# Routed tokens of a two-stage mixture of experts: number and gate scattered as a pair, slot lists loaded as rows and turned by TensorE, token rows of 2048 bytes

## The chip, the cores and the metric

One core of a Trainium2 chip runs the whole kernel. The metric is the device time of one execution in microseconds (us). A run counts as the same when it is within 2% by the verdicts shown with results; the prediction says which smaller difference it holds to be measurable.

## The reference, cut to what matters

Linear attention over 4 x 8 heads gives x, 2304 tokens of 512. A first mixture of 8 experts weights every expert for every token. A second mixture, the part that the change touches, sends each token to one expert only:

```python
logits = xn @ en.T / tau
expert_idx = np.argmax(logits, axis=1)
gate_w = probs[np.arange(N), expert_idx]
for e in range(E):
    mask = expert_idx == e
    h = np.maximum(x[mask] @ w1[e], 0.0)
    out[mask] = gate_w[mask, None] * (h @ w2[e])
```

## The kernel before, in words

The work is written out by hand, in a fixed order on every engine. Attention comes first. Then the first mixture runs as 48 half-stages h, one for each of 16 halves of an expert and each of three batches of 768 tokens (bi = 0, 1, 2); the last three are h = 45, 46 and 47, and each of them finishes the sums of one batch. In the last stages a half-stage has 30 ticks: 14 of `p1_group` (first layer, reading x tiles `xT`, `xB`), then 16 of `p2_plain` (second layer, six matmuls of 384 columns each). Work beside it is hung on ticks: in the list `tail` (L1288 to L1298) tick k means tick k of h = 46 up to 39, and k counts from 40 at the start of h = 47.

**Routing.** Tokens are routed in batches t0 = 0, 6, 12 (in tiles of 128 tokens, six to a batch). For each tile, `route_l` (L883, matmuls L886) makes the logits and `route_a` (L872) turns the tile's sums into rows on TensorE (psum tile psB, one buffer), squares them for the norm and copies them to a row tile (both on ScalarE, L878 and L879). Then `route_b`, `route_o`, `route_c`, `route_s`, `route_d` and `route_w` (L889 to L954) find each token's expert, its slot in the expert's list and its gate. `route_w` writes the gate as element 513 of each row and has SyncE store the rows to `x2d` in DRAM, 513 floats to a token. `route_i` (L956) has GpSimd scatter a tile's token numbers (`tokid`) into the slot list `ids[i]`; there are six lists, one for each tile position i, which are filled beforehand so that the sum over the six is the token number, or NT for an empty slot.

**The table.** `first_blocks` and `other_blocks` (L1018, L1027) turn the counts into a table of blocks (128 slots of one expert): offset, expert, and whether the expert differs from the block before. The first six blocks (NEARLY = 6) are taken from the first two batches, the rest from all.

**The second mixture.** `second(0, 22)` (L1349) runs 22 blocks. For block i, SyncE reads three registers of the table (`load_regs`, L1044) and issues six list loads (`load_ids`, L1053, line L1058), each 128 numbers of 4 bytes, one to a partition. `gather` (L1060) adds the six columns on GpSimd (L1065 to L1067) and has GpSimd gather 128 rows of x2d (L1069) into one of two buffers `xgs`. `tx` turns them (L1111) and splits them into a high part `xth` (ScalarE) and a low part `xtl` (VectorE, L1115), and copies the gate out of the row (`gt`, L1117). `p1` is the first layer: 24 matmuls of 512 columns (L1131 to L1133). `relu` evacuates it (L1141), `th_` turns the hidden values (L1146) and splits them (`hTh` on ScalarE, `hTl` on VectorE, L1150), `p2` is the second layer, 24 matmuls (L1164 to L1166), scaled by the gate into y (L1171) and scattered by GpSimd (L1172).

Weights come in eight chunks of 512 KB for each block, w1 and w2. `wcond` (L1071, line L1074) issues a chunk's load, which moves nothing where the expert is the same. `wsplit` (L1094) casts a chunk on ScalarE (`s1h`, `s2h`, L1102; the last chunk of w2 on GpSimd, L1100) and takes the low half on VectorE (`s1l`, `s2l`, L1103), 1024 columns each. Then the raw tile is free, and the next block's `wcond` of that chunk is issued right after: SyncE's queue follows VectorE's splits. `load_raws` issues the first block's eight chunks; `first_w1(i, cs)` splits w1 chunks of block i and issues those of block i + 1.

The loop of `second` writes, for block i from 2 on, in this order: `p1(i)`; w1 splits of block i + 1; `relu(i)`; `tx(i + 1)`; w2 splits of block i, each followed by `wcond` of block i + 1; for i = 3 alone the rest of the table and `load_ids(6)`; `p2(i - 1)`; `gather(i + 3)`; `th_(i)`. From i = 4 on `load_ids(i + 3)` stands at the head of the turn. Every engine goes through its own part of this order without overtaking.

Of the kernel before, what the change touches and what calls it, by code (L numbers as in the profile page):

```python
# [22 lines left out]
NT = B * S  # L23
# [19 lines left out]
XW = 513  # L43


def build(tc, a, out):
# [30 lines left out]
    c0.tile([P, 16], F32, name="cpad")  # L77
# [10 lines left out]

    x2d = dr.tile([NT + 1, XW], F32, name="x2d")
    ids = [dr.tile([NSLOT, 1], I32, name=f"ids{k}") for k in range(RB)]  # L90
# [174 lines left out]
    sent = wp.tile([P, 1024], I32, tag="wS1_1", name="sent")  # L265
    sents = [sent[:, i * (NSLOT // P):(i + 1) * (NSLOT // P)] for i in range(2)]
    G.memset(sents[0], 0)
    G.memset(sents[1], NT)
    zrow = wp.tile([P, 1024], F32, tag="wA12_1", name="zrow")[0:1, 0:XW]
# [16 lines left out]
    def misc_comp():  # L286
# [4 lines left out]
        V.tensor_copy(iob, itmp3)  # L291
        V.memset(half, 0.5)
# [29 lines left out]
    def load_w(kind, n):  # L322
        if n >= NGR:
            return
        e, g = divmod(n, 2)
        rs = []
        for r_ in range(2):
            t = raw() if kind == 1 or n == 0 else live["h3"].tile([P, 1026 if r_ else 1024], F32, tag=f"rx{r_}", name=f"rx{n}_{r_}")[:, 0:1024]
# [391 lines left out]
    live["h3"].tile([P, 120], F32, name="hpad")  # L720
# [137 lines left out]
    def batch(t0):  # L858
        if t0 not in rt:
            if t0 == TPB:  # L860
                pieces = [live["h3"].tile([P, 2 * TH], F32, tag="r" + q_, name=f"rows{t0}{q_}").unsqueeze(1)[:, :, 0:XW] for q_ in "abcd"]
                pieces += [raw().unsqueeze(1)[:, :, 0:XW] for _ in range(2)]
            else:
                pieces = [live["h3"].tile([P, 2, XW], F32, tag=f"hT{k + 2}", name=f"rows{t0}_{k}") for k in range(TPB // 2)]
            m = TPB // len(pieces)
            rt[t0] = dict(n=TPB, ss=sm.tile([P, 6], F32, tag="ss", bufs=2, name=f"ss{t0}"), rows=[t[:, k] for t in pieces for k in range(m)], pieces=pieces)
        return rt[t0]
# [4 lines left out]
    def route_a(t0, i):  # L872
        r = batch(t0)
        row = r["rows"][i][:, 0:DM]
# [4 lines left out]
        A.copy(row, ps)  # L879

# [63 lines left out]
    def route_w(t0):  # L944
# [105 lines left out]
    idt, idr, xg = {}, {}, {}  # L1050
    xgs = []

    def load_ids(i):  # L1053
        if i not in regs:
            load_regs(i)
        idr[i] = c0.tile([P, RB], I32, tag="idr", bufs=5, name=f"idr{i}")
        for k in range(RB):
            SP.dma_start(out=idr[i][:, k:k + 1], in_=ids[k][bass.ds(regs[i][0], P), :])  # L1058

    def gather(i):  # L1060
        if not xgs:
            xgs.append(live["h3"].tile([P, 2, XW], F32, tag="rx1", name="xgs"))
# [43 lines left out]
    xsp, gt = {}, {}  # L1106

    def tx(i):
# [7 lines left out]
        gt[i] = c0.tile([P, 1], F32, tag="gt", bufs=4, name=f"gt{i}")  # L1116
        V.tensor_copy(gt[i], xg[i][:, DM:DM + 1])  # L1117
# [231 lines left out]
    def second(i0, i1):  # L1349
# [168 lines left out]
```

## Time and profile before

| | us |
|---|---|
| median of 3 runs (lowest, highest) | 2051.58 (2047.44, 2053.9) |
| the profiled execution, its own time | 2048.7 |
| its span in the trace | 2046.8 |
| TensorE busy | 1969.2 (96%) |
| VectorE, ScalarE, GpSimd busy | 1295.8, 869.2, 1055.7 |
| mean granted clock of TensorE | 0.987 |

Times in the rows are microseconds from the start of the span. PE is TensorE, PEld its weight loads, DVE VectorE, ACT ScalarE, POOL GpSimd, SPq the instructions by which SyncE issues DMAs. "[15.69 <-ACT rows L879]" says that the engine stood idle for 15.69 us before the row and which instruction ended that by the profile. A granted clock of 1.00 is 2.4 GHz, 0.50 is 1.2 GHz. The second mixture begins with the row of 1745.76 below and runs to the end; within it TensorE's two layers of one block take about 12.3 us.

### The profile page before, as it was taken

Reading aid. Unit: us, or ns where it says so; the run is one execution under the profiler, and the core shown is the slowest. Engines: PE = TensorE matmul, PEld = TensorE weight load, DVE = VectorE, ACT = ScalarE, POOL = GpSimd, SP = SyncE. Lnnn points to the kernel's source line nnn. Section 1 sums busy time; section 2 is a strip of 40 time slices with the busy share of each in tenths; the row PEclk is TensorE's granted clock in tenths of the full one; section 3 lists DMA queues with packets and bytes.
Section 4 is the critical chain, followed back from the end, with each engine's and each line's share of the span. In section 5 each row is a group of like instructions: output and inputs, shape, how many; then the busy total and the mean of one; then the engine's idle time right before and its main releaser. Section 6 shows DMA issues by size and latency. Waiting matters only on the chain.

```text
span 2046.8 us, 31493 instructions
## 1 busy us (share of the span) xinstructions
PE 1969.2 (96%) x11627; PEld 1888.7 (92%) x11627; DVE 1295.8 (63%) x1838; ACT 869.2 (42%) x1391; POOL 1055.7 (52%) x811
## 2 busy tenths in 40 slices
PE   9999999999999999999999999999999996799998
PEld 8999999999999999999999999999999995578886
DVE  6766556466656655655665665565566453689996
ACT  5566442223332433333342333334233232568785
POOL 1255112666574747656483756647384441345553
PEclk9999999999999999999999999999999997799999
DMA  4344643452725435372634537263543367434861
GB/s 121 111 146 166 227 160 149 141 199 100 249 92 194 157 124 190 108 253 80 212 135 146 180 104 245 85 229 115 166 166 120 119 147 114 63 113 136 298 227 64
DMA packets 138287, 314.63 MB, mean 154 GB/s; under 512 B 30456, under 2 KB 85256, under 8 KB 138130
## 3 DMA queue, kind: packets, MB, share of 16 engines
q1 hardware_dynamic: 134034, 302.06, 45.5%
q0 software_dynamic: 4096, 10.51, 1.7%
q8 instruction: 94, 1.54, 0.3%
q14 instruction: 63, 0.52, 0.1%
HBM read 335.81 MB, written 32.28 MB: 180 GB/s over the span
## 4 chain that ended last, share of the span: by engine, by line
PE 62%; POOL 11%; DVE 9%; issue 8%; DMA 6%; SPq 2%; ACT 2%; POOLq 0%; DVEq 0%; ACTq 0%
PE Q L427 14%; PE Q L426 14%; PE Q L428 14%; DMA rw<-in_moe_w 4%; POOL w1S L346 3%; PE psD L206 3%; DVE s2l L1103 2%; PE psD L426 2%; PE psD L427 2%; POOL hT L474 2%; PE psD L428 2%; PE psA L426 2%; PE psA L428 2%; PE psA L427 2%; POOL w1A L346 2%
## 5 line engine op out<-in xcount | busy, mean ns | idle before, releaser
L490 DVE TENSOR_TENSOR acca<-acca,Q 128x768 f32<-128x768 f32 x182 | 168.7, 951 | 147.2 <-PE Q L428 147.2
L346 POOL TENSOR_TENSOR w1A<-raw,w1A 128x512 fp32r<-128x512 f32 x48 | 61.9, 1289 | 232.2 <-ACT w1A L345 159.2
L426 PE MATMUL Q<-xT,w1S 128*128 128x384 f32 x468 | 156.4, 334 | 0.9 <-ACT ra L495 0.9
L428 PE MATMUL Q<-xT,w1S 128*128 128x384 f32 x468 | 156.4, 334 | 0.0
L427 PE MATMUL Q<-xT,w1S 128*128 128x384 f32 x468 | 156.3, 334 | 0.0
L426 PE MATMUL Q<-hT,w2S 128*128 128x384 f32 x468 | 156.3, 334 | 0.0
L427 PE MATMUL Q<-hT,w2S 128*128 128x384 f32 x468 | 156.3, 334 | 0.0
L428 PE MATMUL Q<-hT,w2S 128*128 128x384 f32 x468 | 156.3, 334 | 0.0
L474 POOL TENSOR_TENSOR hB<-rb,hB 128x768 fp32r<-128x768 f32 x39 | 71.9, 1845 | 136.9 <-ACT hB L471 136.9
L490 DVE TENSOR_TENSOR accb<-accb,Q 128x768 f32<-128x768 f32 x91 | 84.4, 951 | 80.3 <-PE Q L428 80.3
L1103 DVE TENSOR_TENSOR s1l<-rw,s1h 128x1024 fp32r<-128x1024 f32 x88 | 108.8, 1283 | 32.0 <-ACT s1h L1102 31.8
L486 DVE TENSOR_TENSOR Q<-Q,ra 128x768 f32<-128x768 f32 x39 | 37.7, 967 | 124.6 <-PE Q L428 124.6
L495 ACT COPY ra<-Q 128x768 f32<-128x768 f32 x39 | 31.2, 801 | 193.1 <-PE Q L428 156.4
L1102 ACT CAST s1h<-rw 128x1024 fp32r<-128x1024 f32 x88 | 89.0, 1062 | 56.8 <-DMA rw<-in_moe_w 54.6
L426 PE MATMUL Q<-xB,w1A 128*128 128x384 f32 x312 | 104.3, 334 | 0.7 <-DVE accb L843 0.7
L474 POOL TENSOR_TENSOR hT<-ra,hT 128x768 fp32r<-128x768 f32 x39 | 71.4, 1830 | 64.3 <-ACT hT L471 64.3
L428 PE MATMUL Q<-xB,w1A 128*128 128x384 f32 x312 | 104.2, 334 | 0.0
L427 PE MATMUL Q<-xB,w1A 128*128 128x384 f32 x312 | 104.2, 334 | 0.0
L426 PE MATMUL Q<-hB,w2A 128*128 128x384 f32 x312 | 104.2, 334 | 0.0
L427 PE MATMUL Q<-hB,w2A 128*128 128x384 f32 x312 | 104.2, 334 | 0.0
L428 PE MATMUL Q<-hB,w2A 128*128 128x384 f32 x312 | 104.2, 334 | 0.0
L1103 DVE TENSOR_TENSOR s2l<-rw,s2h 128x1024 fp32r<-128x1024 f32 x76 | 92.7, 1262 | 9.4 <-ACT s2h L1102 4.9
(428 smaller groups left out, 6657.2 us busy)
## 6 DMA issues: line engine op xcount, KB each, us to landing
xT<-xpd SPq DMA_DIRECT2D x120, 768.0 KB
rw<-in_moe_w SPq DMA_DIRECT2D x176, 512.0 KB
xB<-xpd SPq DMA_DIRECT2D x90, 768.0 KB
raw<-in_moe_w SPq DMA_DIRECT2D x34, 512.0 KB
gate<-gd SPq DMA_DIRECT2D x45, 384.0 KB
rx<-in_moe_w SPq DMA_DIRECT2D x30, 512.0 KB
xpd<-xT SPq DMA_DIRECT2D x12, 768.0 KB
xpd<-xB SPq DMA_DIRECT2D x9, 768.0 KB
```

What stands on the lines that cost most here:

```text
L206: T.matmul(ps[:, off:off + w], eq[:, sg, h_, ci * P:(ci + 1) * P], kvz[:, h_, sg, o:o + w], start=(sg == 0), stop=(sg == 1))
L346: eng.tensor_tensor(out=t[:, 1], in0=r(nm), in1=f32(t[:, 0]), op=ALU.subtract)
L426: T.matmul(bank, w[:, 0, j, k, :], x[:, 0, k, :], start=start and k == 0, stop=False, skip_group_check=True)
L427: T.matmul(bank, w[:, 0, j, k, :], x[:, 1, k, :], start=False, stop=False, skip_group_check=True)
L428: T.matmul(bank, w[:, 1, j, k, :], x[:, 0, k, :], start=False, stop=stop and k == 1, skip_group_check=True)
L474: eng.tensor_tensor(out=hb[nm][:, 1], in0=src, in1=f32(hb[nm][:, 0]), op=ALU.subtract)
L486: V.tensor_tensor(out=out, in0=x, in1=y, op=op)
L490: V.tensor_tensor(out=z, in0=z, in1=ps, op=op)
L495: A.copy(m1c, b0)
L1102: A.copy(hi, r)
L1103: V.tensor_tensor(out=lo, in0=r, in1=f32(hi), op=ALU.subtract)
```

## The change

- x2d has 512 floats to a row. The gate is no longer in it: `pay` holds for each token the pair (token number, gate) in fp32, and `route_i` scatters pairs into lists of NSLOT x 2 floats. The sentinels that fill the lists are twice as long.
- Rows are stored by `route_a`, as soon as the one or two tiles of a piece are copied; `route_w` only computes the gate.
- A list load brings 128 pairs, 1024 bytes, into one partition; six loads fill six partitions. `gather` adds and turns them with two matmuls against a column of ones into psB, and two copies on VectorE make the number (int32) and the gate. GpSimd's three additions and the gate copy in `tx` go.
- The ticks move: for batch 0 w = 21, d = 23, i from 24; for batch 6 s = 48, w = 49 (before d); the table one tick earlier; the raw loads of w1 at 54 and of w2 at 56; lists 0 and 1 at 57 and 2 and 3 at 69; the first two w1 chunks are split at 68 and 69, the other two in `second`, where the first two gathers and the loads of lists 4 and 5 come first.

```diff
-XW = 513
-    x2d = dr.tile([NT + 1, XW], F32, name="x2d")
-    ids = [dr.tile([NSLOT, 1], I32, name=f"ids{k}") for k in range(RB)]
+    x2d = dr.tile([NT + 1, DM], F32, name="x2d")
+    ids = [dr.tile([NSLOT, 2], F32, name=f"ids{k}") for k in range(RB)]
...
+    pay = c0.tile([P, NTL, 2], F32, name="pay")
...
+        V.tensor_copy(pay[:, :, 0], tokid)
...
     def route_a(t0, i):
...
         A.copy(row, ps)
+        if i % m == m - 1:
+            o = (t0 + i + 1 - m) * P
+            SP.dma_start(out=x2d[o:o + m * P, :].rearrange("(t p) d -> p t d", p=P), in_=r["pieces"][i // m])
...
     def route_w(t0):
...
-        m = n // len(r["pieces"])
-        for k, rows in enumerate(r["pieces"]):
-            V.reciprocal(rows[:, :, DM], se[:, m * k:m * k + m])
-            o = (t0 + m * k) * P
-            SP.dma_start(out=x2d[o:o + m * P, :].rearrange("(t p) d -> p t d", p=P), in_=rows)
+        V.reciprocal(pay[:, t0:t0 + n, 1], se)
...
-        G.indirect_dma_start(out=ids[i], out_offset=bass.IndirectOffsetOnAxis(si[:, i:i + 1], 0), in_=tokid[:, t0 + i:t0 + i + 1], in_offset=None)
+        G.indirect_dma_start(out=ids[i], out_offset=bass.IndirectOffsetOnAxis(si[:, i:i + 1], 0), in_=pay[:, t0 + i, :], in_offset=None)
...
     def load_ids(i):
...
-        idr[i] = c0.tile([P, RB], I32, tag="idr", bufs=5, name=f"idr{i}")
+        idr[i] = live["h3"].tile([P, 2 * TH], F32, tag="r" + "abcd"[i % 4], name=f"idr{i}")[0:RB, 0:2 * P]
         for k in range(RB):
-            SP.dma_start(out=idr[i][:, k:k + 1], in_=ids[k][bass.ds(regs[i][0], P), :])
+            SP.dma_start(out=idr[i][k:k + 1, :], in_=ids[k][bass.ds(regs[i][0], P), :].rearrange("p o -> (p o)").unsqueeze(0))
...
     def gather(i):
...
-        r = idr.pop(i)
+        r = idr.pop(i).rearrange("k (p o) -> k o p", o=2)
+        ps = psum("B", [P, 2])
+        for o in range(2):
+            T.matmul(ps[:, o:o + 1], r[:, o, :], ones[0:RB, 0:1], start=True, stop=True)
         idt[i] = c0.tile([P, 1], I32, tag="idt", bufs=5, name=f"idt{i}")
-        G.tensor_tensor(out=r[:, 0:3], in0=r[:, 0:3], in1=r[:, 3:6], op=ALU.add)
-        G.tensor_tensor(out=r[:, 0:1], in0=r[:, 0:1], in1=r[:, 1:2], op=ALU.add)
-        G.tensor_tensor(out=idt[i], in0=r[:, 0:1], in1=r[:, 2:3], op=ALU.add)
+        V.tensor_copy(idt[i], ps[:, 0:1])
+        gt[i] = c0.tile([P, 1], F32, tag="gt", bufs=5, name=f"gt{i}")
+        V.tensor_copy(gt[i], ps[:, 1:2])
...
     def tx(i):
...
-        gt[i] = c0.tile([P, 1], F32, tag="gt", bufs=4, name=f"gt{i}")
-        V.tensor_copy(gt[i], xg[i][:, DM:DM + 1])
...
-    tail = route_steps(0, (2, 4, 6, 8, 10, 12), (1, 2, 3, 4, 5, 6), p=13, b=14, o=16, s=18, c=19, d=21, w=23, i=(23, 23, 24, 25, 26, 27))
-    tail += route_steps(6, (26, 28, 40, 43, 45, 47), (25, 26, 27, 42, 43, 44), p=47, b=46, o=47, c=49, d=49, i=(50, 50, 50, 51, 53, 54), s=50, w=52)
-    tail += [(k, partial(next, rf, None)) for k in (51, 52, 53, 54, 56)] + [(55, partial(load_regs, i)) for i in range(2)]
-    tail += [(55, partial(load_raws, 1, range(4))), (55, partial(load_raws, 2, range(4))), (56, early_second), (56, start_second)]
-    tail += [(65 + 2 * c, partial(first_w1, 0, (c,))) for c in range(3)]
-    tail += [(63 if i < 2 else 67, partial(load_ids, i)) for i in range(NEARLY)]
-    tail += [(67, partial(gather, 0)), (68, partial(gather, 1))]
+    tail = route_steps(0, (2, 4, 6, 8, 10, 12), (1, 2, 3, 4, 5, 6), p=13, b=14, o=16, s=18, c=19, w=21, d=23, i=(24, 24, 25, 25, 26, 27))
+    tail += route_steps(6, (26, 28, 40, 43, 45, 47), (25, 26, 27, 42, 43, 44), b=46, p=47, o=47, s=48, c=49, w=49, d=49, i=(50, 50, 50, 51, 53, 54))
+    tail += [(k, partial(next, rf, None)) for k in (50, 51, 52, 53, 55)] + [(54, partial(load_regs, i)) for i in range(2)]
+    tail += [(54, partial(load_raws, 1, range(4))), (55, early_second), (55, start_second)]
+    tail += [(56, partial(load_raws, 2, range(4)))]
+    tail += [(68 + c, partial(first_w1, 0, (c,))) for c in range(2)]
+    tail += [(57 if i < 2 else 69, partial(load_ids, i)) for i in range(4)]
...
         if i0 == 0:
             t0 = NA
-            first_w1(0, (3,))
+            for k in range(2):
+                gather(k)
+                load_ids(k + 4)
             for k in range(3, NTL - NA):
                 route_l(t0, k)
                 route_a(t0, k)
+                if k < 5:
+                    first_w1(0, (k - 1,))
```

## Rows read from the trace of the kernel before

**Rows 1.** Busy time by stretch (us), granted clock, DMA share, GB/s; all engines.
```profile
1700.00:1725.00 25.00, 11.87 (x74) 11.51 (x74) 3.71 (x9) 0.00 (x0) 1.68 (x2) 0.83 0.97 89
1725.00:1730.00 5.00, 1.99 (x10) 1.99 (x11) 1.23 (x1) 3.03 (x7) 0.00 (x0) 0.50 1.02 415
1860.00:1910.00 50.00, 50.00 (x249) 41.65 (x247) 50.00 (x51) 40.49 (x53) 25.03 (x25) 1.00 0.36 108
```
**Rows 2.** TensorE in order of time: start, us, [idle before <- releaser].
```profile
1707.84 0.95 PE L886 MATMUL psC<-enT,accb 128*128 128x8 f32 x8
1708.65 0.42 PE L426 MATMUL psD<-hB,w2A 128*128 128x384 f32 x1
...
1728.01 1.11 PE L877 MATMUL psB<-ident,accb 128*128 128x128 f32 x4 [15.69 <-ACT rows L879]
...
1745.76 0.78 PE L1131 MATMUL psA<-s1h,xth 128*128 128x512 f32 x1
...
1763.12 1.11 PE L1146 MATMUL psD<-ident,hr 128*128 128x128 f32 x4 [8.09 <-ACT hr L1141]
...
1796.98 0.79 PE L1132 MATMUL psA<-s1h,xtl 128*128 128x512 f32 x1 [4.60 <-DVE gt L1117]
...
1801.77 0.40 PE L1131 MATMUL psA<-s1h,xth 128*128 128x512 f32 x1
1802.00 0.40 PE L1132 MATMUL psA<-s1h,xtl 128*128 128x512 f32 x1
...
1810.44 0.60 PE L1146 MATMUL psD<-ident,hr 128*128 128x128 f32 x4
```
**Rows 3.** ScalarE in order of time.
```profile
1725.71 1.04 ACT L1102 CAST s1h<-rw 128x1024 fp32r<-128x1024 f32 x1 [27.21 <-DMA rw<-in_moe_w]
1726.66 0.59 ACT L878 ACTIVATE rows<-psB 128x512 f32<-128x512 f32 x1
...
1727.37 0.59 ACT L879 COPY rows<-psB 128x512 f32<-128x512 f32 x1
...
1758.69 1.99 ACT L1102 CAST s1h<-rw 128x1024 fp32r<-128x1024 f32 x2 [10.07 <-DMA rw<-in_moe_w]
```
**Rows 4.** The chain that ended last, in order of time: start, us, what.
```profile
1698.85 25.71 DMA x2d<-raw
...
1724.68 10.94 DMA rw<-in_moe_w
...
1817.85 0.33 SPq L1058
```
**Rows 5.** SyncE's queue in order of time.
```profile
1704.22 20.80 SPq L1074 DMA_DIRECT2D rw<-in_moe_w  x8
...
1738.32 0.53 SPq L1074 DMA_DIRECT2D rw<-in_moe_w  x2
1740.78 17.44 SPq L1058 DMA_DIRECT2D idr<-ids  x24
1758.60 1.34 SPq L1074 DMA_DIRECT2D rw<-in_moe_w  x4
...
1815.05 7.86 SPq L1058 DMA_DIRECT2D idr<-ids  x12
...
1941.82 5.38 SPq L1058 DMA_DIRECT2D idr<-ids  x6
```
**Rows 6.** VectorE in order of time, around block 3.
```profile
1796.25 0.68 DVE L1115 TENSOR_TENSOR xtl<-psA,xth 128x512 fp32r<-128x512 f32 x1
...
1809.17 3.48 DVE L1103 TENSOR_TENSOR s2l<-rw,s2h 128x1024 fp32r<-128x1024 f32 x3
```
**Rows 7.** GpSimd in order of time.
```profile
1820.02 0.32 POOL L1065 TENSOR_TENSOR idr<-idr 128x3 int32<-128x3 int32 x1 [6.48 <-DMA idr<-ids]
```
**Rows 8.** All work on two tiles, ids and idr: durations in ns, min/median/max.
```profile
DMA to landing us min/median/max: 5.1/8.5/20.7
...
L1066 POOL TENSOR_TENSOR idr<-idr x22: 191/1052/1191, 1737.5 to 2002.3; 128x1 int32<-128x1 int32 x22
```

More of the change, by code (lines that the diff above doesn't have):

```diff
@@ L76, in build @@
     G.affine_select(out=ident, in_=ident, pattern=[[-1, P]], compare_op=ALU.not_equal, fill=1.0, base=0, channel_multiplier=1)
-    c0.tile([P, 16], F32, name="cpad")
+    c0.tile([P, 32], F32, name="cpad")
     hp = top.enter_context(tc.tile_pool(name="hp", bufs=1, side="right"))
@@ L248, in build @@
     onesb = c0.tile([P, P], BF16, name="onesb")
-    itmp = wp.tile([P, 1024], I32, tag="wS2_1", name="itmp")[:, 0:8]
+    ramps = wp.tile([P, 1024], I32, tag="wS4_1", name="ramps")
+    itmp, itmp2 = ramps[:, 0:8], ramps[:, 8:16]
     G.iota(itmp, [[1, 8]], base=-8, channel_multiplier=0)
     iom8 = c0.tile([P, 8], F32, name="iom8")
-    itmp2 = wp.tile([P, 1024], I32, tag="wS4_1", name="itmp2")[:, 0:8]
     G.iota(itmp2, [[REG, 8]], base=0, channel_multiplier=0)
     ereg = c0.tile([P, 8], F32, name="ereg")
-    tokid = c0.tile([P, NTL], I32, name="tokid")
+    tokid = wp.tile([P, 1024], I32, tag="wS1_1", name="tokid")[:, 512:512 + NTL]
+    pay = c0.tile([P, NTL, 2], F32, name="pay")
     G.iota(tokid, [[P, NTL]], base=-NT, channel_multiplier=1)
@@ L264, in build @@
     total = c0.tile([1, 1], I32, name="total")
[L265 to L269, printed above, removed]
+    sent = wp.tile([P, 1024], F32, tag="wS2_1", name="sent")
+    NSP = NSLOT // P * 2
+    sents = [sent[:, 512 * i:512 * i + NSP] for i in range(2)]
+    G.memset(sents[0], 0.0)
+    G.memset(sents[1], 0.0)
+    G.memset(sents[1].rearrange("p (c o) -> p c o", o=2)[:, :, 0], float(NT))
+    zrow = wp.tile([P, 1024], F32, tag="wA12_1", name="zrow")[0:1, 0:DM]
     G.memset(zrow, 0.0)
@@ L327, in load_w @@
         for r_ in range(2):
-            t = raw() if kind == 1 or n == 0 else live["h3"].tile([P, 1026 if r_ else 1024], F32, tag=f"rx{r_}", name=f"rx{n}_{r_}")[:, 0:1024]
+            t = raw() if kind == 1 or n == 0 else live["h3"].tile([P, 1024], F32, tag=f"rx{r_}", name=f"rx{n}_{r_}")
             SP.dma_start(out=t, in_=a[f"moe_w{kind}"][e, g, r_])
@@ L719, in build @@
     live["h3"] = top.enter_context(tc.tile_pool(name="h3", bufs=1, reuse_waits="tile"))
-    live["h3"].tile([P, 120], F32, name="hpad")
+    live["h3"].tile([P, 128], F32, name="hpad")
     m1 = st.enter_context(tc.tile_pool(name="m1", bufs=1, reuse_waits="tile"))
@@ L860, in batch @@
             if t0 == TPB:
-                pieces = [live["h3"].tile([P, 2 * TH], F32, tag="r" + q_, name=f"rows{t0}{q_}").unsqueeze(1)[:, :, 0:XW] for q_ in "abcd"]
-                pieces += [raw().unsqueeze(1)[:, :, 0:XW] for _ in range(2)]
-            else:
-                pieces = [live["h3"].tile([P, 2, XW], F32, tag=f"hT{k + 2}", name=f"rows{t0}_{k}") for k in range(TPB // 2)]
-            m = TPB // len(pieces)
-            rt[t0] = dict(n=TPB, ss=sm.tile([P, 6], F32, tag="ss", bufs=2, name=f"ss{t0}"), rows=[t[:, k] for t in pieces for k in range(m)], pieces=pieces)
+                pieces = [live["h3"].tile([P, 2 * TH], F32, tag="r" + q_, name=f"rows{t0}{q_}").unsqueeze(1)[:, :, 0:DM] for q_ in "abcd"]
+                pieces += [raw().unsqueeze(1)[:, :, 0:DM] for _ in range(2)]
+            else:
+                pieces = [live["h3"].tile([P, 2, DM], F32, tag=f"hT{k + 2}", name=f"rows{t0}_{k}") for k in range(TPB // 2)]
+            rt[t0] = dict(n=TPB, ss=sm.tile([P, 6], F32, tag="ss", bufs=2, name=f"ss{t0}"), pieces=pieces)
         return rt[t0]
@@ L873, in route_a @@
         r = batch(t0)
-        row = r["rows"][i][:, 0:DM]
+        m = TPB // len(r["pieces"])
+        row = r["pieces"][i // m][:, i % m]
         ps = psum("B", [P, DM])
@@ L1048, in load_regs @@
         regs[i] = (off, ev, fv)
-    idt, idr, xg = {}, {}, {}
+    idt, idr, xg, gt = {}, {}, {}, {}
     xgs = []
@@ L1055, in load_ids @@
             load_regs(i)
-        idr[i] = c0.tile([P, RB], I32, tag="idr", bufs=5, name=f"idr{i}")
+        idr[i] = live["h3"].tile([P, 2 * TH], F32, tag="r" + "abcd"[i % 4], name=f"idr{i}")[0:RB, 0:2 * P]
         for k in range(RB):
-            SP.dma_start(out=idr[i][:, k:k + 1], in_=ids[k][bass.ds(regs[i][0], P), :])
+            SP.dma_start(out=idr[i][k:k + 1, :], in_=ids[k][bass.ds(regs[i][0], P), :].rearrange("p o -> (p o)").unsqueeze(0))
     def gather(i):
         if not xgs:
-            xgs.append(live["h3"].tile([P, 2, XW], F32, tag="rx1", name="xgs"))
-        r = idr.pop(i)
+            xgs.append(live["h3"].tile([P, 2, DM], F32, tag="rx1", name="xgs"))
+        r = idr.pop(i).rearrange("k (p o) -> k o p", o=2)
+        ps = psum("B", [P, 2])
+        for o in range(2):
+            T.matmul(ps[:, o:o + 1], r[:, o, :], ones[0:RB, 0:1], start=True, stop=True)
         idt[i] = c0.tile([P, 1], I32, tag="idt", bufs=5, name=f"idt{i}")
-        G.tensor_tensor(out=r[:, 0:3], in0=r[:, 0:3], in1=r[:, 3:6], op=ALU.add)
-        G.tensor_tensor(out=r[:, 0:1], in0=r[:, 0:1], in1=r[:, 1:2], op=ALU.add)
-        G.tensor_tensor(out=idt[i], in0=r[:, 0:1], in1=r[:, 2:3], op=ALU.add)
+        V.tensor_copy(idt[i], ps[:, 0:1])
+        gt[i] = c0.tile([P, 1], F32, tag="gt", bufs=5, name=f"gt{i}")
+        V.tensor_copy(gt[i], ps[:, 1:2])
         xg[i] = xgs[0][:, i % 2, :]
@@ L1104, in wsplit @@
         w2t[which, i, c] = (hi, lo)
-    xsp, gt = {}, {}
+    xsp = {}
     def tx(i):
```

## The prediction

> **What bounds the kernel now.** I read the busy time by stretch first, then each engine in order of time where TensorE is idle, then the chain that ended last. Almost everywhere TensorE is the bound: the steady second stage shows 50.00 us busy of 50.00 at granted clock 1.00, beside a VectorE that is as full [rows 1]. The exception is the passage from the first stage to the second, 1700 to 1800: in its first 25 us TensorE works 11.87 us while the DMA engines are 0.97 busy at only 89 GB/s [rows 1]. Three holes are to be seen: 15.69 us before 1728.01, 8.09 before 1763.12, 4.60 before 1796.98 [rows 2].
>
> The first hole names ScalarE's row copy, but ScalarE itself waited 27.21 us for the first raw weights [rows 3], and the chain shows why: the stores of routed rows (25.71 us), then the weights behind them (10.94) [rows 4]. The second hole is ScalarE again, 10.07 us of waiting for a chunk [rows 3]; that load carried nothing (block 1 has block 0's expert), but SyncE reached it only at 1758.60, after 24 list loads that took 17.44 us [rows 5]. The third is VectorE's backlog after these delays.
>
> **The change, part by part.** The sum is made against the profiled execution's own 2048.7 us (span 2046.8 and 1.9 around it); the median of the runs stands 2.9 above it.
>
> *Row stores out of the way.* Six stores of batch 6 leave from tick 26 on, as each row is copied, not together at tick 52. At the old rate (25.71/6 = 4.3 us each, [rows 4]) or at 415 GB/s (0.6 us, [rows 1]) they are done before the first weight load, which left at 1704.22 [rows 5] and waits for the block table, not for them. So the shorter row is worth nothing here. The stores of batch 0 share the DMA engines with x tiles needed 25 us later: nothing; were that cover gone, three stores of two rows cost 26 us at the old rate.
>
> *VectorE before tick 55.* The gate sum and the exponent come earlier, the table one tick earlier. Six small operations (the gate's sum, the table's first columns) now stand ahead of the first-stage evacuations at ticks 51 and 52; each costs less than the 0.68 us of a 512-column one [rows 6], I take 0.17: +1.0 us, between 0 and 4.
>
> *New end of stage one.* TensorE stopped at 1728.01 - 15.69 = 1712.3 [rows 2]. Left were 18 matmuls of 384 columns (0.23 x 384/512 = 0.17 each), eight transposes and eight narrow matmuls (0.81/8 = 0.10 each, [rows 2]): 4.7 us, so 1717.0, with VectorE's 1.0 1718.0. The third row's transposes end 12 matmuls earlier, at 1715.9; its evacuation takes 1.3 us, two casts 1.04 each [rows 3], two low halves 1.16 each [rows 6] with one accumulate between: chunk 1 of block 0 is split at about 1721.5. SyncE by then has issued eight loads from 1704 (4.2 MB, 10 us at 415 GB/s) and twelve lists of about 0.5 us each.
>
> *List loads.* Still six issues per block, and their order is unchanged: lists 2 to 5 stand before chunks 2 and 3 of block 1. From the end of the second load to that chunk it was 1758.60 - 1738.85 = 19.75 us [rows 5]; with half a us for one store now between, SyncE reaches it at 1742.0, ScalarE follows at once as before. **Gain 16.6 us**, carried by everything behind it. Two TensorE waits lie beside this: the gathers of blocks 2 and 3 now stand before p1 of block 0 and need lists 2 and 3, so p1 starts near 1733 (1745.76 before, [rows 2]), still in time. Bounds: a scatter of the pair may take 20.7 us to land instead of 8.5 [rows 8], which delays lists 0 and 1 and leaves 9.6; 24 issues at the 0.27 of the cheapest load [rows 5] would give 22.
>
> *The list now passes through TensorE.* Before, GpSimd waited for it; now TensorE does, in program order, and VectorE behind it with the two copies. For block 6 the trace has the wait already: GpSimd stood 6.48 us, until 1820.02 [rows 7]. Its list is asked for after the second layer's weights of block 3 are split (1809.17 + 3.48 = 1812.65, [rows 6]); register reads bring the first issue to 1815.05 [rows 5], the last ends at 1818.18 [rows 4], landing 1.8 later. TensorE passes this place at 1810.44, before block 3's hidden transposes [rows 2]. Nobody noticed while only GpSimd waited. Now block 3's transposes, p1 of block 4 and p2 of block 3 queue behind: **a new hole of 9.6 us**. Both ends hang on the same event, block 3's activations split at 1796.25 [rows 6], so an earlier start does not shrink it. A clock loss follows: after the 4.60 us hole eleven matmuls took 4.79 us (1796.98 to 1801.77) where 0.23 each at full clock makes 2.5 [rows 2]: 2.3 us at the lower level. Bounds for both: 0 and 13.
>
> *Two matmuls per gather.* Sixteen gathers (blocks 6 to 21) lie where TensorE has no idle time. The trace has no matmul of one column from six partitions; the nearest is 128x8, 0.10 us: 16 x 2 x 0.10 = 3.2 us. Below, 0; above, twice that. I take the row. The Trainium skill, "TensorE: Matmul & The Clock Gate", section "Wait — 56ns, not 53.3ns?", puts the floor for small matmuls at about 25 ns; by it the term would be an estimated 0.8 us, and no run here shows one so cheap.
>
> *GpSimd's additions go.* Three per block; nobody waits for them in the steady stage. The second takes 1052 ns in the median but 191 at the least [rows 8], so GpSimd is the one that waits, and VectorE gains nothing in my sum. The Trainium skill, "SBUF — State Buffer", section "SBUF: two separate sides", has it that GpSimd and a VectorE operation with two SBUF inputs lock each other out, whoever starts first winning; by it VectorE could also win back something, estimated at most 2 x 3 x 0.2 = 1.2 us over two early gathers. It is part of the first rival.
>
> *Start.* Sentinels double, 0.47 MB more, 1.1 us of transfers early in the attention; taken as 0, at most 1.1.
>
> Sum: -16.6 + 9.6 + 2.3 + 3.2 = -1.5, that is 2047.2, and on the scale of the medians **2050.1 us**: no change.
>
> **Rivals.**
> *The list of block 6 comes in time.* Then -16.6 + 3.2 = -13.4: 2038.2. For it: VectorE, which asks for the list, loses some work and contention. Against it: from 1796.25 VectorE needs 16.4 us to the list's request and TensorE 14.2 to its place [rows 2, 6], and the list itself 7.4 more; nearly 10 us would have to go. Chance 0.26.
> *Every list is late (slower).* Place: TensorE's gather matmul in blocks 9 to 21. Price: where weights are really loaded, the six issues stretch to 5.38 us [rows 5], and the list would land about 3 us after TensorE's place; eight such blocks at 1.4 on average are 11 us: 2061. It decides once VectorE finishes a block's weights over 5 us after that block's hidden transposes. Against it: the hole at block 6 lets VectorE catch up. Chance 0.15.
> *The change does not clear the path.* Scatters of pairs land late or stores linger, so the early gain is about 9: 2057.7. Against: nothing else is on the DMA engines then. Chance 0.11.
>
> **How the numbers follow.** The forecast has 0.48, with 2044 to 2056 as its own range. A measurement tells about 0.3% (6.2 us) from no change. Faster: the first rival and 0.04 of the forecast's tail, 0.30. Slower: 0.15, half of the third, which stands on the bound, and 0.015 of the forecast's tail, 0.22. Within: 0.48. The range 2038 to 2060 reaches the first rival and the third and cuts most of the second.
>
> **What would show it.** Right: no hole before 1728, p1 of block 0 near 1733 and of block 1 near 1746; SyncE's 24 list loads unchanged at about 17 us; then a TensorE idle of 8 to 11 us ended by a list's DMA before block 3's hidden transposes, the clock down after it; about 0.2 us per gather; no further list waits. The forecast is wrong if that hole is missing, if holes recur block after block, or if the first weights still wait.

## The result, and the profile after

The changed kernel takes **2061.55 us** (median of 4 runs, 2060.28 to 2063.68) against 2050.1 of the kernel before, run beside it: ratio 1.0053, with an interval of 1.0035 to 1.0071. On another chip, with later experiments, it was 1.0032 (1.0019 to 1.0044). It is slower by a third to half a per cent; the forecast was no change, 2050.1, and its range ended at 2060.

The profiled execution took 2061.3 us (span 2059.2; 2046.8 before). Busy time by stretch, for [rows 1]: length, busy TensorE, its weight loads, VectorE, ScalarE, GpSimd, granted clock, DMA share, GB/s.

```profile
1700.00:1725.00 25.00, 20.45 (x122) 20.02 (x121) 8.96 (x21) 6.22 (x12) 3.17 (x4) 0.91 0.71 168
1725.00:1750.00 25.00, 20.08 (x81) 17.98 (x82) 6.90 (x14) 9.46 (x16) 6.38 (x5) 0.55 0.24 77
1800.00:1850.00 50.00, 41.18 (x192) 33.93 (x191) 36.88 (x41) 30.29 (x39) 10.72 (x9) 0.90 0.45 159
1850.00:1900.00 50.00, 50.00 (x249) 41.16 (x248) 46.57 (x52) 38.61 (x51) 13.15 (x12) 1.00 0.29 96
```

The old gap of 1700 to 1725 is largely filled. From 1725 to 1750 the granted clock is 0.55 (0.64 before), near its lower level, after two waits that are shown next. There is a new gap after 1800, and the steady stretch is as full as before: what is lost there is work, not waiting. TensorE in order of time, for [rows 2]:

```profile
1725.36 0.98 PE L1068 MATMUL psB<-ones,idr 6*128 6x1 f32 x4 [4.91 <-DMA idr<-ids]
1730.36 0.98 PE L1068 MATMUL psB<-ones,idr 6*128 6x1 f32 x4 [4.02 <-DMA idr<-ids]
...
1743.43 0.80 PE L1134 MATMUL psA<-s1h,xth 128*128 128x512 f32 x1
...
1753.65 0.66 PE L1149 MATMUL psD<-ident,hr 128*128 128x128 f32 x4 [1.24 <-ACT hr L1144]
...
1809.96 0.98 PE L1068 MATMUL psB<-ones,idr 6*128 6x1 f32 x4 [8.82 <-DMA idr<-ids]
1810.88 1.12 PE L1149 MATMUL psD<-ident,hr 128*128 128x128 f32 x4
...
1864.58 0.63 PE L1068 MATMUL psB<-ones,idr 6*128 6x1 f32 x4
1865.13 0.66 PE L1149 MATMUL psD<-ident,hr 128*128 128x128 f32 x4
...
1877.57 0.63 PE L1068 MATMUL psB<-ones,idr 6*128 6x1 f32 x4
1878.13 0.66 PE L1149 MATMUL psD<-ident,hr 128*128 128x128 f32 x4
```

Three things are to be seen. The 15.69 us before 1728.01 and the 8.09 before block 0's hidden transposes are gone, but TensorE now stands for lists 0 and 1 (4.91 and 4.02). At block 6's gather it stands 8.82 us. And from one block's hidden transposes to the next (the period of a block, in what follows) it is 13.00 us with a gather between (1865.13 to 1878.13); before it was 12.30 (1822.74 to 1835.04), about as it is here where the last blocks have no gather (2008.06 to 2020.41: 12.35). The two rows of before:

```profile
1822.74 0.60 PE L1146 MATMUL psD<-ident,hr 128*128 128x128 f32 x4
...
1835.04 0.60 PE L1146 MATMUL psD<-ident,hr 128*128 128x128 f32 x4
```

SyncE's queue after the change, for [rows 5]:

```profile
1705.53 5.50 SPq L1079 DMA_DIRECT2D rw<-in_moe_w  x8
1715.88 12.12 SPq L1060 DMA_DIRECT2D idr<-ids  x12
1728.10 0.41 SPq L885 DMA_DIRECT2D x2d<-rows  x1
1728.85 0.54 SPq L1079 DMA_DIRECT2D rw<-in_moe_w  x2
1731.85 16.38 SPq L1060 DMA_DIRECT2D idr<-ids  x24
1748.33 0.41 SPq L885 DMA_DIRECT2D x2d<-rows  x1
1749.12 0.53 SPq L1079 DMA_DIRECT2D rw<-in_moe_w  x2
```

The twelve loads of lists 0 and 1 stretch over 12.12 us. SyncE's waits, summed from 1695 to 1760 (waiting line, releaser: us, times, longest), say why: eight of the twelve wait for one of the eight raw loads, each for the one eight places ahead of it in the queue.

```profile
SPq L1060 <- DMA rw<-in_moe_w: 11.5, 8, 4.6
```

The raw loads are slow at first: two-microsecond stretches, GB/s last.

```profile
1706.00:1708.00 2.00, 2.00 (x14) 2.00 (x13) 0.56 (x1) 0.00 (x0) 0.00 (x0) 1.00 1.94 33
1710.00:1712.00 2.00, 2.00 (x16) 2.00 (x16) 0.56 (x1) 0.00 (x0) 0.00 (x0) 1.00 0.90 39
1714.00:1716.00 2.00, 2.00 (x17) 1.96 (x16) 0.00 (x0) 0.89 (x3) 0.00 (x0) 1.00 0.91 342
1718.00:1720.00 2.00, 2.00 (x15) 2.00 (x14) 0.52 (x1) 1.57 (x4) 0.00 (x0) 1.00 1.05 424
```

The DMA engines are busy and move a tenth of what they move later.

The end of stage one differs by up to 3.6 us between profiles of one kernel (first raw load at 1705.53 and 1701.95 in the two of the changed kernel), so landmarks are compared **from the first raw load on**. The 12.4 us between the spans come about so:

| stretch | before | after | difference |
|---|---|---|---|
| start to first raw load | 1704.22 | 1705.53 | +1.3 |
| to block 0's hidden transposes | 58.90 | 48.12 | -10.8 |
| to block 2's | 27.99 | 28.66 | +0.7 |
| to block 4's | 31.63 | 43.84 | +12.2 |
| to block 19's | 185.37 | 194.26 | +8.9 |
| to the end | 38.69 | 38.79 | +0.1 |

(Hidden transposes of blocks 0, 2, 4, 19: before 1763.12, 1791.11, 1822.74, 2008.11; after 1753.65, 1782.31, 1826.15, 2020.41.)

### The profile page after: what moved, and what is told of

Its sections match the earlier page's. It is cut to its first block, busy times and chain, and to the rows that moved or that the text cites. A ratio compares the mean times of both kernels' runs of the same rounds, so it can differ in the third digit from the quotient of the medians.

```text
span 2059.2 us, 31662 instructions
## 1 busy us (share of the span) xinstructions
PE 1986.0 (96%) x11715; PEld 1901.7 (92%) x11715; DVE 1305.4 (63%) x1852; ACT 869.9 (42%) x1391; POOL 1002.2 (49%) x746
## 4 chain that ended last, share of the span: by engine, by line
PE 74%; POOL 10%; issue 6%; DVE 5%; DMA 2%; ACT 2%; SPq 1%; DVEq 0%; POOLq 0%; ACTq 0%
PE Q L430 14%; PE Q L429 14%; PE Q L431 14%; PE psD L205 3%; POOL w1S L349 3%; PE psD L429 2%; POOL hT L477 2%; PE psD L430 2%; PE psD L431 2%; PE psA L429 2%; PE psA L1135 2%; PE psA L1134 2%; PE psA L431 2%; PE psA L1136 2%; PE psA L430 2%
## 5 line engine op out<-in xcount | busy, mean ns | idle before, releaser
L1108 DVE TENSOR_TENSOR s1l<-rw,s1h 128x1024 fp32r<-128x1024 f32 x88 | 102.5, 1220 | 15.8 <-ACT s1h L1107 13.5
L1108 DVE TENSOR_TENSOR s2l<-rw,s2h 128x1024 fp32r<-128x1024 f32 x76 | 99.5, 1357 | 9.9 <-ACT s2h L1107 9.0
L477 POOL TENSOR_TENSOR hT<-rd,hT 128x768 fp32r<-128x768 f32 x39 | 72.2, 1850 | 44.5 <-ACT hT L474 44.5
```

Source lines behind the costliest of these rows:

```text
L477: eng.tensor_tensor(out=hb[nm][:, 1], in0=src, in1=f32(hb[nm][:, 0]), op=ALU.subtract)
L1108: V.tensor_tensor(out=lo, in0=r, in1=f32(hi), op=ALU.subtract)
```

## The experiments

Each is an edit of the changed kernel. The kernel before ran beside them all and had medians from 2050.1 to 2055.7 on the chips used, so ratios to it are compared, not times. The base:

> The changed kernel once more, beside the two below on one chip, as their base: ratio 1.0035 to 1.0071 to the kernel before.

Measured: 2059.83 us, 1.0032 (1.0019 to 1.0044), a little under the first interval's lower end. Waits at gathers 0 and 1 of 5.72 and 3.88 us, 9.18 at block 6, period 12.99.

### The hole at block 6

```
-            if i + 3 < i1:
+            if i + 2 == NEARLY:
+                gather(NEARLY)
+            if i + 3 < i1 and i + 3 != NEARLY:
                 gather(i + 3)
```

> Changed kernel with block 6's gather moved one block later, behind block 3's second layer, beside the gather of block 7; nothing else. Theory (the changed kernel pays 8.82 us where TensorE stands at that gather, and some 2.4 us of half clock behind it): the 8.82 us wait for a list is gone, block 4's hidden transposes come near 1815 instead of 1826.15, and the whole is about 11 us shorter than the changed kernel, near 2050.5. Rival (VectorE's backlog of that moment is only covered by the hole): another wait, on a split or on a low half, opens within two blocks, at most 4 us are won, 2057 or more.

Measured: 1.0003 (0.9993 to 1.0012), 2053.62 us. From the first raw load to block 4's hidden transposes 110.5 us, 10.1 less than the 120.6 of the changed kernel, as the theory has it. The next block then lost 2.9 (15.92 for 13.00): its rows came 1.11 late, and from about 1817.1 to 1820.6 the granted clock was 0.50, which costs some 1.7. That followed a wait of 1.19 before block 4's hidden transposes, where the second of two adjacent gathers stood for VectorE's copies of the first. So the rival has a part too.

```
             early = i + 3 > NEARLY
+            if i + 3 == NEARLY:
+                for _ in ob:
+                    pass
+                load_ids(i + 3)
...
-            if i + 3 == NEARLY:
-                for _ in ob:
-                    pass
-                load_ids(i + 3)
```

> Changed kernel with the list of block 6 asked for at the start of block 3 instead of at its end, ahead of block 3's weight loads on SyncE's queue; the gather stays where it was. Theory (the list is late only because its six loads stand on SyncE's queue behind weight loads that wait for VectorE's splits; the block table that they need was written near 1785): the 8.82 us wait and the half clock after it are gone, block 4's hidden transposes come near 1815 instead of 1826.15, and the whole is 10 to 11 us shorter than the changed kernel, about as long as the kernel before (ratio 0.999 to 1.001), a little under the run with the later gather, whose rows came 1.11 us late. Rival (the list cannot come earlier, because the table or the buffer of list 2 is late, as the prediction had it when it let both ends hang on one event): the wait stays above 5 us, ratio 1.003 or more.

Measured: 0.9973 (0.9964 to 0.9982), 2050.36 us, below the ratio expected. The trace's own difference to block 19 is 9.3 and 10.6 us against the two profiles of the changed kernel. SyncE's queue and TensorE:

```profile
1796.33 2.64 SPq L1060 DMA_DIRECT2D idr<-ids  x6
```
```profile
1802.88 0.63 PE L1068 MATMUL psB<-ones,idr 6*128 6x1 f32 x4
1803.44 0.66 PE L1149 MATMUL psD<-ident,hr 128*128 128x128 f32 x4
...
1815.88 0.63 PE L1068 MATMUL psB<-ones,idr 6*128 6x1 f32 x4
```

Asked for at 1796.33, the list is there at the gather: no wait stands in brackets, and from block 2's to block 4's hidden transposes it is 31.69 us again (31.63 before; two gathers are in it now, and a wait of 3.15 us stands where it was 4.60). So the hole came from the place of six loads in a queue.

### The price of turning a list

```
-        for o in range(2):
+        for o in (0, 1, 0, 1):
             T.matmul(ps[:, o:o + 1], r[:, o, :], ones[0:RB, 0:1], ...)
```

> Changed kernel with the two turning matmuls of every gather issued twice into the same place; nothing else. Theory (each fp32 pair costs 0.55 us of TensorE's time in the steady stage): the period goes from 13.00 to 13.55 us, in all 16 gathers x 0.55 = 8.8 us more, near 2070. Rival (the 0.70 us of each gather are a fixed price of breaking the stream of matmuls, with its copies and waits, and the matmuls are cheap): 16 x 0.2 = 3 us more, near 2065, period about 13.2.

Measured: 1.0078 (1.0064 to 1.0092), 2068.67 us.

```profile
1864.83 1.10 PE L1068 MATMUL psB<-ones,idr 6*128 6x1 f32 x8
1865.86 0.66 PE L1149 MATMUL psD<-ident,hr 128*128 128x128 f32 x4
...
1878.29 1.10 PE L1068 MATMUL psB<-ones,idr 6*128 6x1 f32 x8
```

The period is 13.46 us (1864.83 to 1878.29), between the two expectations: two matmuls more cost 0.46, 0.23 each. Of the first pair's 0.70, 0.24 is left for standing in the stream. One fp32 matmul is two records (x4 for two, x8 for four), 0.115 us apiece. The starts in the changed kernel divide the 0.24: 0.08 more than before between the second layer's last matmul and what follows it (0.32, 1864.26 to 1864.58), 0.09 in the gather's own 0.55 (1864.58 to 1865.13), and 0.07 in the first transposes behind it (0.50 for 0.43). The weight loads go with that: the transposes' weights begin to load 0.23 us ahead of them in the kernel before (1872.15 for 1872.38), but together with them behind a gather (1865.13).

```
-            SP.dma_start(out=idr[i][k:k + 1, :], in_=ids[k][bass.ds(regs[i][0], P), :]...)
+            SP.dma_start(out=idr[i][:, 2 * k:2 * k + 2], in_=ids[k][bass.ds(regs[i][0], P), :])
...
-        for o in range(2):
-            T.matmul(ps[:, o:o + 1], ...)
+        G.tensor_tensor(out=r[:, 0:6], in0=r[:, 0:6], in1=r[:, 6:12], op=ALU.add)
+        G.tensor_tensor(out=r[:, 0:2], in0=r[:, 0:2], in1=r[:, 2:4], op=ALU.add)
+        G.tensor_tensor(out=r[:, 0:2], in0=r[:, 0:2], in1=r[:, 4:6], op=ALU.add)
-        V.tensor_copy(idt[i], ps[:, 0:1])
+        G.tensor_copy(idt[i], r[:, 0:1])
-        V.tensor_copy(gt[i], ps[:, 1:2])
+        G.tensor_copy(gt[i], r[:, 1:2])
```

> Changed kernel with its lists loaded as columns of pairs and added up by GpSimd, three additions and two copies per gather; the pair, the 2048-byte rows, the early stores and the ticks all stay. Theory (what the change loses, it loses by turning lists on TensorE): the block period of the steady stretch returns from 13.00 to 12.30 us, the 8.82 us hole at block 6 and its half clock are gone, the list waits of gathers 0 and 1 pass to GpSimd and block 0's transposes still wait for the rows, so about 20 us are won: near 2041, faster than the kernel before by 0.4%. Rival (the period comes from the two VectorE copies or from the longer wait of the pair's second column, not from TensorE): the period stays at 12.8 or more and the time above 2050.

Measured: **0.9954** (0.994 to 0.9967), 2042.45 us: faster than both. Period and first hole:

```profile
1753.78 1.12 PE L1149 MATMUL psD<-ident,hr 128*128 128x128 f32 x4 [11.37 <-ACT hr L1144]
...
1866.11 0.60 PE L1149 MATMUL psD<-ident,hr 128*128 128x128 f32 x4
...
1878.40 0.60 PE L1149 MATMUL psD<-ident,hr 128*128 128x128 f32 x4
```

The period is 12.29 us again. By itself this does not part TensorE's matmuls from VectorE's two copies, since both are gone here. The run before does, with twice the matmuls and the same copies, and so does the order of events in the changed kernel: the copies of the gather at 1838.59 come after TensorE has gone on to the transposes.

```profile
1839.15 0.66 PE L1149 MATMUL psD<-ident,hr 128*128 128x128 f32 x4
```
```profile
1840.09 0.15 DVE L1070 CAST idt<-psB 128x1 int32<-128x1 f32 x1
```

So the rival is out, and the 0.70 came from TensorE. GpSimd now waits for the list of block 6 (7.38 us), and TensorE only 2.14 for its rows. The 11.37 us are the old second hole [rows 2], in a new place: block 1's chunk stands behind 24 list loads of 18.18 us on SyncE's queue.

### The early gain

```
-    tail += [(56, partial(load_raws, 2, range(4)))]
     tail += [(57 if i < 2 else 69, partial(load_ids, i)) for i in range(4)]
+    tail += [(57, partial(load_raws, 2, range(4)))]
```

> Changed kernel with the loads of lists 0 and 1 issued ahead of the four raw loads of the second layer instead of behind all eight raw loads; nothing else. Theory (lists 0 and 1 are late because each list load waits for a raw load eight places ahead of it, and the raw loads start slowly): the waits of 4.91 and 4.02 us at gathers 0 and 1 shrink to under 3 together, the 24 later list loads start some 4 us earlier, block 1's hidden transposes or its first layer come near 1749.5 instead of 1753.65, and 3 to 4 us remain to the end, near 2058. Rival (another thing holds block 0 there: its splits or the rows' gather): the waits shrink but the later landmarks move by less than 1 us, 2061.

Measured: 1.0041 (1.0027 to 1.0055). The theory fell in its consequence: the wait at gather 0 shrank to 0.75 us and that at gather 1 stayed 3.98, but lists 2 and 3, now eight places behind the moved raw loads, made TensorE wait 2.29 and 3.35, and block 0's hidden transposes came 50.1 us after the first raw load (48.1 and 49.2 in the changed kernel). (The row at 1753.65, which the expectation calls block 1's, is that of block 0's hidden transposes; they stand within block 1's first layer. The same holds for the 1758 in the expectation with rows of 513 columns below.)

```
-    tail += route_steps(6, ..., d=49, i=(50, 50, 50, 51, 53, 54))
+    tail += route_steps(6, ..., d=49, i=())
...
-        V.tensor_copy(idt[i], ps[:, 0:1])
+        V.tensor_scalar_min(idt[i], ps[:, 0:1], ...)
```

> Changed kernel that leaves out the six scatters of the second batch of 768 tokens (those tokens get no place in a list; the token numbers of early gathers are limited to the rows stored). Theory (the raw loads start at some 40 GB/s for 8 us because the scatters' small writes are still being made): the eight raw loads move over 300 GB/s from their second microsecond on and lists 0 and 1 land some 7 us earlier. Rival (the first packets of the weights are slow by themselves): 30 to 60 GB/s for 8 us as before.

Measured once, 2054.26 us. Two-microsecond stretches, SyncE's raw loads, then TensorE:

```profile
1706.00:1708.00 2.00, 2.00 (x13) 2.00 (x12) 0.48 (x2) 0.00 (x0) 0.00 (x0) 1.00 0.99 356
1710.00:1712.00 2.00, 2.00 (x16) 2.00 (x15) 0.18 (x1) 0.00 (x0) 0.00 (x0) 1.00 1.02 399
1718.00:1720.00 2.00, 2.00 (x13) 1.75 (x11) 0.00 (x0) 1.97 (x5) 0.00 (x0) 1.00 0.01 2
```
```profile
1704.01 5.20 SPq L1079 DMA_DIRECT2D rw<-in_moe_w  x8
```
```profile
1719.80 0.63 PE L1068 MATMUL psB<-ones,idr 6*128 6x1 f32 x4
...
1746.96 0.66 PE L1149 MATMUL psD<-ident,hr 128*128 128x128 f32 x4 [1.75 <-ACT hr L1144]
```

Without the scatters the raw loads run at 356 to 420 GB/s from 1706 to 1716 but for one stretch (252), no wait for a list is left at the first two gathers, and block 0's hidden transposes come 42.95 us after the first raw load: 15.95 less than before, nearly the 16.6 forecast.

```
+    def touch():
+        for w in (1, 2):
+            for c in range(4):
+                SP.dma_start(out=cpad[...], in_=a[f"moe2_w{w}"][0, c, :, 0:2])
+    tail += [(44, touch)]
```

> Changed kernel that reads 8 bytes of each row of expert 0's second-stage weights some 15 us before the raw loads, into a spare tile. Theory (the scatters slow the raw loads): no difference, some 40 GB/s for 8 us from 1706. Rival (the first access to these rows is slow, whoever makes it): the small reads take long, and the raw loads then move over 300 GB/s from the start, lists 0 and 1 land some 7 us earlier, and 4 us or more are won at block 1.

Measured once, 2061.03 us: the small reads were issued from 1681.92 on, the raw loads still ran at 23 to 61 GB/s from 1706 to 1712, and it was 48.2 us to block 0's hidden transposes. A first access to these rows is not what is slow.

Which part brought the gain that is there? Four runs on the stores:

```
-    x2d = dr.tile([NT + 1, DM], F32, name="x2d")
+    x2d = dr.tile([NT + 1, DM + 1], F32, name="x2d")
...
+        A.copy(r["pieces"][i // m][:, i % m, DM:DM + 1], ps[:, 0:1])
```

> Changed kernel with rows of 513 columns (2052 bytes) again in x2d, in the row tiles and in what the gathers read; the last column carries a copy of a number that nobody uses (one ScalarE copy of one column per tile more), and the gate still comes with the list; the stores leave as early as in the changed kernel. Theory (the length of a row costs nothing where the stores are early): the same as the changed kernel within 2 us, landmarks of block 0 and 1 within 1 us. Rival (a store of rows of 2052 bytes takes 4.3 us, so the length of the row is what cleared the path): stores linger, the raw loads end 5 us or more later and block 1's hidden transposes come at 1758 or later.

Measured: 1.0045 (1.003 to 1.006), 50.5 us: 1.3 to 2.4 more than the two profiles of the changed kernel, outside the 1 us expected, with a median 2.8 us above that of the base (2 expected), and far from the rival.

```
-        if i % m == m - 1:
+        if i % m == m - 1 and t0 != TPB:
...
+    tail += [(52, partial(stores, 6))]
```

> Changed kernel whose six stores of the second batch's rows (2048 bytes a row) leave together at tick 52, as in the kernel before, and not as each row is copied. Theory (the early leaving clears the path, not the shorter row): the stores fall into the slow stretch behind the scatters, the eight raw loads end 6 us or more later, the hole at gather 0 grows beyond 10 us (4.91 and 5.72 in the two profiles of the changed kernel), and from the first raw load to block 0's hidden transposes it is 55 us or more (48.1 and 49.2); the ratio goes from 1.003 to 1.005 to 1.006 or more. Rival (rows of 2048 bytes move fast whenever they leave): 50 us or less, the ratio unchanged.

Measured: 1.003 (1.002 to 1.004). This told nothing of late stores: they left at 1670.7 to 1688.6 as before the edit (1670.6 to 1689.0), because SyncE stood at them already and waited only for the copied rows. That alone is worth knowing: it is the gate's leaving the row that sets the stores free, not the moved line.

```
+            V.tensor_copy(rows[:, 0, 0:1], rows[:, 0, 0:1])
             SP.dma_start(out=x2d[...], in_=rows)
```

> Changed kernel whose six stores of the second batch's rows (2048 bytes a row) wait at tick 52 for a VectorE operation (one number of each row block copied onto itself, six operations), as they waited for the gate's column in the kernel before; merely issuing them at tick 52 had left them at 1670.7 to 1688.6, since SyncE was there early. Theory (what cleared the path is that the stores leave ahead of the scatters, at 1670 to 1689 instead of 1696 to 1699): they fall into the slow stretch behind the scatters, the raw loads end 5 us or more later, the waits for lists 0 and 1 grow beyond 13 us together (8.9 and 9.6 in the two profiles of the changed kernel), from the first raw load to block 0's hidden transposes it is 54 us or more (48.1 and 49.2), the ratio 1.005 or more. Rival (rows of 2048 bytes are through in time even then): 51 us or less from the first raw load to these transposes, and only the six operations, 1 us, are lost: 1.0035 to 1.004.

Measured: 1.0036 (1.0022 to 1.005). Stores at 1699.0 to 1702.1, and 46.95 us: the theory fell, short rows get through even late.

```profile
1706.93 7.61 SPq L1085 DMA_DIRECT2D rw<-in_moe_w  x8
```
```profile
1704.00:1706.00 2.00, 2.00 (x13) 2.00 (x12) 0.56 (x1) 0.00 (x0) 0.36 (x1) 1.00 1.23 25
1708.00:1710.00 2.00, 2.00 (x13) 2.00 (x12) 0.56 (x1) 0.00 (x0) 0.00 (x0) 1.00 0.68 253
```

The slow stretch is there all the same, but it fell mostly on the stores and was over 1 to 2 us after the first raw load, which itself left later; so part of it is not in the 46.95. Counted from the last scatter of the batch, block 0's hidden transposes come after 50.5 us here, 49.6 and 50.6 in the changed kernel.

> Changed kernel with both at once: rows of 2052 bytes, and the six stores tied to a VectorE operation at tick 52. The lists, the pair and the other ticks are those of the changed kernel. Each alone left the way from the first raw load to block 0's hidden transposes where it was (50.5 us with long rows stored early, 46.95 with short rows stored late; 48.1 and 49.2 in the changed kernel; 58.9 in the kernel before). Theory (either of the two is enough; only long rows that leave behind the scatters are slow): 55 us or more, TensorE waits over 13 us for lists 0 and 1 together, ratio 1.006 or more. Rival (neither counts, and the gain came from the new ticks and the list loads): 51 us or less, 1.0035 to 1.005.

(The edits of the run with rows of 513 columns and of the run with tied stores, together.) Measured: 1.0083 (1.007 to 1.0097), 2069.38 us, 56.2 us to block 0's hidden transposes, or 59.8 from the last scatter. SyncE, then TensorE, then two stretches:

```profile
1697.76 0.32 SPq L892 DMA_DIRECT2D x2d<-rows6a  x1
...
1705.70 18.64 SPq L1086 DMA_DIRECT2D rw<-in_moe_w  x8
```
```profile
1732.52 0.98 PE L1075 MATMUL psB<-ones,idr 6*128 6x1 f32 x4 [14.52 <-DMA idr<-ids]
```
```profile
1714.00:1716.00 2.00, 2.00 (x15) 1.96 (x16) 0.48 (x1) 0.96 (x5) 0.00 (x0) 1.00 1.08 64
1718.00:1720.00 2.00, 0.00 (x1) 0.00 (x0) 0.00 (x0) 0.00 (x0) 0.00 (x0) 1.00 1.07 78
```

This is the picture of the kernel before: the eight issues stretch to 18.64 us (20.80 in [rows 5]). Only rows of 2052 bytes that leave among the scatters hold the raw loads up that long; the change removes both conditions, and either would have done nearly as well.

### A version that beats both

GpSimd's additions, the early list of block 6, and this:

```
                 gather(k)
-                load_ids(k + 4)
...
                     first_w1(0, (k - 1,))
+            for k in range(2):
+                load_ids(k + 4)
```

> The version with GpSimd's additions, with the list of block 6 asked for at the start of block 3, and with lists 4 and 5 loaded after the last two chunks of block 1's first layer instead of before them. Theory: in the version with GpSimd's additions TensorE's largest hole, 11.37 us before block 0's hidden transposes, is a chunk that SyncE loads only at 1749.26, behind 24 list loads of 18.18 us; twelve fewer ahead of it bring it some 8 us earlier, and the early list of block 6 takes away the 2.14 us wait for its rows and its half clock, 3 us: together 8 to 11 us under that version, near 2033, faster than both kernels. Rival (lists 2 and 3, or VectorE's backlog, hold the same place): the chunk moves and the hole stays above 7 us, 2038 or more.

Measured: **0.9882** (0.9862 to 0.9903), 2031.47 us. TensorE:

```profile
1743.90 0.66 PE L1149 MATMUL psD<-ident,hr 128*128 128x128 f32 x4
...
1805.87 0.60 PE L1149 MATMUL psD<-ident,hr 128*128 128x128 f32 x4
...
1818.16 0.60 PE L1149 MATMUL psD<-ident,hr 128*128 128x128 f32 x4
```

No wait stands before block 0's hidden transposes, and the period is 12.29 from block 3 on. How much of it is order alone:

> Changed kernel with the lists still turned on TensorE, with the two moves of loads of the combined version: block 6's list asked for at the start of block 3, lists 4 and 5 behind the last chunks of block 1's first layer. Theory (the period of 13.00 us stays, and block 0 is held by its lists on TensorE, so that the earlier chunk finds only the 1.24 us wait before block 0's hidden transposes): 0 to 2 us under the version with the early list alone, ratio 0.996 to 0.998, 17 us or more above the combined version. Rival (the chunk is worth its 8 us here too): ratio 0.9935 or less.

Measured: 0.9959 (0.9944 to 0.9973), 2044.76 us, at the edge of what the theory has: 47.85 us to block 0's hidden transposes, 0.3 and 1.3 under the changed kernel, and 0.0014 or 2.9 us under the version with the early list alone (0 to 2 expected). The step from there to the combined version is 0.0077 or 15.8 us (17 or more expected). It is the price of turning on TensorE with what belongs to it, since the form of the list loads and the engine of the two copies change along: 8.2 us up to block 0's hidden transposes and 9.85 from block 4's to block 19's, less what the combined version gives back between.

## Why the prediction was wrong, point by point

The bound and the places were read rightly. Two terms of the sum were mis-sized, both to the optimistic side: the price of the matmuls and the rate of the first raw loads.

**Two matmuls per gather: the larger error.** The step took 0.10 us for a matmul "128x8", from a row of eight records [rows 2]. Those eight records are four fp32 matmuls of two records each, so the same row says 0.20, and even the upper bound, twice the row, gave only 6.4 us. Measured are 0.70 per gather: 2 x 0.23 for the matmuls and 0.24 for breaking the stream, a term that the sum did not have. From block 4 to block 19 that is 14 gathers and 9.8 us, of which +8.9 show, since the kernel before lost 0.9 there in two longer periods; the sum had 3.2 for all sixteen. The floor that the prediction quoted from the Trainium skill, "TensorE: Matmul & The Clock Gate", section "Wait — 56ns, not 53.3ns?", made it an estimated 0.8 us; the runs, with 0.115 us for each record, speak against using it as the price of fp32 matmuls. That several passes are needed is in the Trainium skill, "FP8 and Floating Point Precision", section "TensorE Precision Notes", which gives four for true fp32; this trace shows two records.

**The early gain: 10.8 and 9.7 instead of 16.6.** The step that failed is "eight loads from 1704 (4.2 MB, 10 us at 415 GB/s)". They took 18 us, in the first eight microseconds at 33 to 41 GB/s, so lists 0 and 1 were waited for and block 0's first layer began at 1743.43, not near 1733. The 24 later list loads took 16.38 us, as forecast. The rate came from the end of the old transfer [rows 1]; the slow stretch of the same view, 89 GB/s, was laid to the stores alone. The run without the second batch's scatters gives 15.95, so the rest of that step held. The prediction had named the danger, pairs that land late, and its price, a gain of 9.6, but it looked for it in the landing time: the pairs landed in 3.8 to 5.1 us, faster than before [rows 8], and the loads behind them were slow all the same.

```profile
DMA to landing us min/median/max: 3.8/4.5/5.1
```

The third rival, "the change does not clear the path" (2057.7), has the size of this loss, but neither of its conditions: no scatter landed late and no store lingered.

**VectorE before tick 55, +1.0:** +1.3 in one profile and -2.3 in the other, within what the end of stage one varies by.

**The hole at block 6, 9.6 + 2.3: right.** 8.82 (9.18 in the second profile) before block 3's hidden transposes, and half clock after it, 1809.96 to about 1815.7; from block 2 to block 4 +12.2 in all, with the price of two gathers in it. That an earlier start would not shrink it was right too: it is 8.78 in the run without scatters, where block 0's hidden transposes came 6.7 us sooner; an earlier place in SyncE's queue removes it.

**"The shorter row is worth nothing here": right, for this change.** With early stores it is worth 1.3 to 2.4 us; with late ones it would have been worth the 9.3 us between 46.95 and 56.2.

**GpSimd's additions go, nothing gained:** right. GpSimd is busy 13.15 us of 50 instead of 25.03 [rows 1], and TensorE is full in both.

**Rivals.** "Every list is late" is out: no list is waited for after block 6, but for one wait of 0.53 us in the second profile (at 1953.26). Its time, 2061, was nearly met by luck: what was lost went to matmuls and to the early part, not to waits block after block. "The list of block 6 comes in time" did not happen.

Replaced by what was measured, the sum is -10.8 + 12.2 + 0.7 + 8.9 + 1.3 + 0.1 = +12.4, the difference of the spans.

## What to carry to other kernels

Work moved onto the bounding engine is paid in full and at every turn, however small: count the instructions that one call really issues (records of the trace, not calls), and add something for breaking its stream. Where an engine that nobody waited for hands a wait to the one that everybody waits for, look how late that wait ends, and for the queue place that makes it late. A transfer's rate is taken from the stretch in which it will run: ask what has just been on the queues, not only what is on them.

## What was not expected of the hardware

Six scatters of 128 pairs of 8 bytes (the last issued at 1704.04, landed within some 5 us) leave the weight loads behind them at 33 to 41 GB/s until 1714, with the DMA share at 0.42 to 1.94 and no scatter packet in the trace from 1706 on; without the scatters it is 356 from 1706 on, with one stretch of 252. The slow stretch falls on whatever transfers come then, on row stores in the run with tied stores (25 to 43 GB/s from 1702 to 1708), and it does not end at a fixed time after the last scatter: 10 us after its issue in the changed kernel, about 5 there. The Trainium skill, "DMA: Bandwidth & Descriptors", section "Specifications", says that transfers under 512 bytes are made by reading, changing and writing back; the run without scatters fits that small writes cost much, but why later transfers are slow when the writes have landed no run here shows.

Rows of 2052 bytes that leave among the scatters make the passage 7 to 9 us longer (56.2 against 49.2, 48.1 and 46.95); earlier they cost 1.3 to 2.4, and at 2048 bytes late stores cost nothing that shows. By the same page of the Trainium skill, section "How a descriptor splits into AXI transactions", each transaction starts at a 256-byte boundary, so a row of 2052 bytes takes nine where an aligned one of 2048 takes eight, an estimated eighth more. For six stores of 0.6 us each at the 415 GB/s of [rows 1] that would be an estimated half a microsecond; what was measured is much more, and only in this place. Why the two act together stays open.
